# A gated feed-forward kernel: the mirrored value matmul moved between gate and value of the next unit, and a row broadcast done by DMA in place of a matmul

## The chip, the cores and the metric

The kernel runs on one core of one Trainium2 chip. The metric is the time on the device in microseconds (us), as the median of several executions. A profile is one execution; its span (first to last instruction) is about 1.8 us shorter than the time of that execution. I compare ratios to runs of the kernel before made in the same rounds on the same chip, and give the 95% interval.

PE is TensorE's matmul, ACT is ScalarE, DVE is VectorE, POOL is GpSimd, SP is the engine whose queue issues most DMAs.

## The reference

```python
def reference(x, w_gate, w_val, w_out):        # x: 8 x 3008 x 256, float32
    X = np.fft.fft(np.fft.fft(x, axis=1), axis=2).real
    t = X.reshape(8 * 3008, 256)
    g = t @ w_gate                             # 256 x 1536
    silu = g * (1.0 / (1.0 + np.exp(-g)))
    return (silu * (t @ w_val)) @ w_out        # 1536 x 256
```

The kernel folds the second transform into the weights. The first one has a mirror symmetry along the sequence: a column of coefficients P and one of Q give the row k ("plus", P and Q added) and the row M-k ("minus", P and Q subtracted). So one pass over half of the sequence gives both.

## The kernel before

The half sequence is cut into 24 tiles of up to 512 columns, and the 1536 hidden features into 12 blocks of 128. A *unit* is (tile t, block f). For every unit PE makes in PSUM the gate `g` (two matmuls), from which ACT takes the silu for the plus row. A third matmul with `Wm` (it is -2 times `Wq`, but zero for feature row 0) adds onto the same bank and turns `g` into the mirrored gate, and ACT takes its silu too. The value is done the same way in an ordinary unit. In a *split* unit (f = 0, 2, 3, 5, 7, 9 of tiles 2 to 20; 9 of 12 blocks in tiles 21 and 22) the even part `e` and the odd part `o` go to two banks; DVE combines them into both values, and GpSimd, not DVE, multiplies silu and value. As `Wm` leaves out row 0, DVE must add that row of Q times a weight. It needs that row in all 128 partitions: `bc`.

```python
    psG = ctx.enter_context(tc.tile_pool(name="psG", bufs=3, space=bass.MemoryType.PSUM))
    psV = ctx.enter_context(tc.tile_pool(name="psV", bufs=3, space=bass.MemoryType.PSUM))
    # [...]
    def part_a(u):                                    # L700 on
        # [...]
        mm(g, Wp, 0, Pt, True, False)                 # L716 is inside mm
        mm(g, Wq, 0, Qt, False, True)
        if split(u):
            e = psV.tile([P, T], F32, name="v"); mm(e, Wp, 1, Pt, True, True)
            o = psV.tile([P, T], F32, name="v"); mm(o, Wm, 1, Qt, True, True)
            # sg = silu(g) on ACT (L728);  es = bc * w0 + e (DVE, L731)
            # vp = -0.5 * o + es (DVE, L733);  vm = 0.5 * o + es, reversed (DVE, L735)
            # hp = sg * vp (GpSimd, L736)
            return
        # else: v (two matmuls), sg = silu(g) (ACT, L743), hp = sg * v (DVE, L744)

    def part_b(u):
        # gate: one mirror matmul onto g (L753); unless split: one onto v (L753)
        # split: silu (ACT, L757), hm = silu * vm (GpSimd, L758)
        # else:  silu (ACT, L761), hm = silu * v (DVE, L762)
    # [...]
    for i, u in enumerate(units):
        t, f = u
        if f == 0 and split((t, SPLIT[0])):
            ps = psG.tile([P, T], F32, name="g")
            nc.tensor.matmul(ps[:, :w], sel, pq_tiles(t)[1][:, :w], start=True, stop=True)   # L856
            bc[t] = bcp.tile([P, T], F32, name="bc")
            nc.scalar.copy(bc[t][:, :w], ps[:, :w])                                          # L859
        # [...]
        part_a(u)
        if owork:
            owork.run(4)          # 4 matmuls of the output product of the tile before (L676)
        if prev is not None:
            part_b(prev)          # the mirror of the unit BEFORE
        # [...] 4 more output matmuls; then GpSimd's steps that fold the input of later
        # tiles, and the transforms that fill P and Q of later tiles
        prev = u
```

After every 24 output matmuls ACT copies a bank out (`ev`, L682), which falls into the first four of the units 3, 6, 9 and 0.

Of the kernel before, what the change touches and what calls it, by code (L numbers as in the profile page):

```python
# [12 lines left out]
F32 = mybir.dt.float32  # L13
I32 = mybir.dt.int32
BF16 = mybir.dt.bfloat16
AF = mybir.ActivationFunctionType
Alu = mybir.AluOpType
# [14 lines left out]
def kernel(  # L32
# [8 lines left out]
    nc = tc.nc  # L41
    B, M, D = x.shape
    Dff = moe_w_gate.shape[1]
    P = 128
# [4 lines left out]
    nF = Dff // P  # L49
    T = 512  # L50
# [6 lines left out]
    nT = len(wide)  # L57
# [9 lines left out]
    def width(t):  # L67
        return wide[t]

    def tile_of(c):  # L70
        return max(t for t in range(nT) if t0[t] <= c)
# [6 lines left out]
    psG = ctx.enter_context(tc.tile_pool(name="psG", bufs=3, space=bass.MemoryType.PSUM))  # L78
# [6 lines left out]
    Wm = const.tile([P, 2, Dff], BF16, name="Wm")  # L85
# [5 lines left out]
    sel = const.tile([P, P], BF16, name="sel")  # L91
# [22 lines left out]
    def rows_at(b, row, ap):  # L114
        return bass.AP(tensor=x.tensor, offset=(b * M + row) * D, ap=ap)
# [4 lines left out]
    def down_set(b, a, j, L, n):  # L120

        return rows_at(b, R * (a + 1) - 2 * j, [[2 * L * D, n], [-2 * D, L], [1, 2 * D]])
# [3 lines left out]
    def load_a(b, q):  # L126
        X3 = XA.rearrange("p a q d -> p a (q d)")
        return ([lambda h=h: q.dma_start(out=X3[LA * h:LA * (h + 1), 0:4, :],
                                         in_=up_block(b, JA - LA * h, LA)) for h in range(NA)] +
                [lambda a=a: q.dma_start(out=X3[:, 4 + a, :], in_=down_set(b, a, JA, LA, NA)) for a in range(4)])  # L130
# [99 lines left out]
    for hi in range(2):  # L230
        q.dma_start(out=XC3[64 * hi:64 * hi + NCR, 0:2, :],
                    in_=rows_at(0, 2 * (P + 1) - 1 + 2 * hi * R, [[2 * D, NCR], [R * D, 2], [1, 2 * D]]))
    for hi in range(2):
        for a in range(2):
            q.dma_start(out=XC3[64 * hi:64 * hi + NCR, 2 + a, :],
                        in_=down_set(0, 3 - 2 * hi - a, JC, LC, NC_))
    q.dma_start(out=XC0[NCR:64 + NCR + 1:64, 0:2, 1],
                in_=rows_at(0, 0, [[2 * R * D, 2], [R * D, 2], [1, D]]))
# [21 lines left out]
    for i in range(6):  # L260
        ps = psO.tile([P, T], F32, name="o")
# [99 lines left out]
    opposite(0)  # L361
    nc.vector.memset(EOf[:, 1, :, P:P + 1], 0.0)
    nc.vector.memset(Tab[:, :, :, :, NOO - 1:NOO], 0.0)
    nc.vector.memset(sel[0:1, :], 1.0)
    vts(m2, pcol, scalar1=0.0, scalar2=-2.0, op0=Alu.not_equal, op1=Alu.mult)
    vts(sgn, half, scalar1=1.0 / 32, scalar2=1.0, op0=Alu.mult, op1=Alu.add)
    vts(wC, pc, scalar1=float(LC - 1), scalar2=-0.5, op0=Alu.is_equal, op1=Alu.mult)
# [146 lines left out]
    def pq_tiles(t):  # L514
        if t not in ptile:
            w = width(t) + B if t == nT - 1 else T
            ptile[t] = (pqp if t < nT - 1 else const).tile([P, w], BF16, name="Pt")
            qtile[t] = (pqp if t < nT - 1 else const).tile([P, w], BF16, name="Qt")
        return ptile[t], qtile[t]
# [78 lines left out]
    def whole_part(b, part):  # L598
        transform(b, part, (0,))
        transform(b, part, (1,))  # L600
# [15 lines left out]
    sgp = ctx.enter_context(tc.tile_pool(name="sg", bufs=3))  # L616
    sgv = ctx.enter_context(tc.tile_pool(name="sgv", bufs=4))
    esp = ctx.enter_context(tc.tile_pool(name="es", bufs=2))
    bcp = ctx.enter_context(tc.tile_pool(name="bc", bufs=2))
# [73 lines left out]
    hts = {}  # L693
    state = {}
    owork = None

    SPLIT = (0, 2, 3, 5, 7, 9)
    SPLIT_END = (0, 1, 2, 4, 5, 7, 8, 10, 11)
    t_end = tile_of((B - 1) * H) + 1

    bc = {}

    def split(u):

        return 2 <= u[0] < nT - 1 and u[1] in (SPLIT if u[0] < t_end else SPLIT_END)

    def part_a(u):
        t, f = u
        w = width(t) + (B if t == nT - 1 else 0)
        fs = slice(f * P, (f + 1) * P)  # L710
        if f == 0:
            hts[t] = (hp.tile([P, nF, T + B], BF16, name="hp"), hp.tile([P, nF, T], BF16, name="hm"))
        Pt, Qt = pq_tiles(t)

        def mm(ps, Wt, gv, src, start, stop):
            nc.tensor.matmul(ps[:, :w], Wt[:, gv, fs], src[:, :w], start=start, stop=stop,  # L716
                             skip_group_check=True)

        g = psG.tile([P, T], F32, name="g")
        mm(g, Wp, 0, Pt, True, False)  # L720
        mm(g, Wq, 0, Qt, False, True)
        if split(u):
            e = psV.tile([P, T], F32, name="v")
            mm(e, Wp, 1, Pt, True, True)
            o = psV.tile([P, T], F32, name="v")
            mm(o, Wm, 1, Qt, True, True)
            sg = sgv.tile([P, T], F32, name="sgv")
            nc.scalar.activation(sg[:, :w], g[:, :w], AF.Silu)  # L728
            stt = nc.vector.scalar_tensor_tensor
            es = esp.tile([P, T], F32, name="es")  # L730
            stt(es[:, :w], bc[t][:, :w], w0[:, f:f + 1], e[:, :w], op0=Alu.mult, op1=Alu.add)  # L731
            vp = vvp.tile([P, T], F32, name="vv")
            stt(vp[:, :w], o[:, :w], -0.5, es[:, :w], op0=Alu.mult, op1=Alu.add)  # L733
            vm = vvp.tile([P, T], F32, name="vv")
            stt(vm[:, w - 1::-1], o[:, :w], 0.5, es[:, :w], op0=Alu.mult, op1=Alu.add)  # L735
            nc.gpsimd.tensor_tensor(hts[t][0][:, f, :w], sg[:, :w], vp[:, :w], op=Alu.mult)  # L736
            state[u] = (g, vm)
            return
        v = psV.tile([P, T], F32, name="v")
        mm(v, Wp, 1, Pt, True, False)  # L740
        mm(v, Wq, 1, Qt, False, True)
        sg = sgp.tile([P, T], F32, name="sg")
        nc.scalar.activation(sg[:, :w], g[:, :w], AF.Silu)  # L743
        nc.vector.tensor_tensor(hts[t][0][:, f, :w], sg[:, :w], v[:, :w], op=Alu.mult)  # L744
        state[u] = (g, v)

    def part_b(u):
        t, f = u
        w = width(t)
        Pt, Qt = pq_tiles(t)  # L750
        g, v = state.pop(u)
        for gv, ps in ((0, g), (1, v))[:1 if split(u) else 2]:
            nc.tensor.matmul(ps[:, :w], Wm[:, gv, f * P:(f + 1) * P], Qt[:, :w], start=False, stop=True,  # L753
                             skip_group_check=True)
        if split(u):
            sg = sgv.tile([P, T], F32, name="sgv")
            nc.scalar.activation(sg[:, w - 1::-1], g[:, :w], AF.Silu)  # L757
            nc.gpsimd.tensor_tensor(hts[t][1][:, f, :w], sg[:, :w], v[:, :w], op=Alu.mult)  # L758
            return
        sg = sgp.tile([P, T], F32, name="sg")  # L760
        nc.scalar.activation(sg[:, :w], g[:, :w], AF.Silu)  # L761
        nc.vector.tensor_tensor(hts[t][1][:, f, w - 1::-1], sg[:, :w], v[:, :w], op=Alu.mult)  # L762


    slot = {(b, part): max(first_tile[(b, part)] - 1, 0) * nF + 4 for b, part in jobs}
# [10 lines left out]
    for b in range(2, B, 2):  # L776
        u = slot[(b, 0)] - 1
# [8 lines left out]
    def run_loads(n):  # L786
        for _, fn in loads[:n]:
            fn()
        del loads[:n]

    def fold_step(what, i, unit):
        kind, b = what
        q, j = divmod(i, 7)
        if i == 0:
            run_loads(max((k + 1 for k, (w_, _) in enumerate(loads) if w_ == what), default=0))
        if j == 0:
            if kind == "A":
                queue[what] = fold_steps(nc.gpsimd, XA, *coef_a(b), q, slice(0, P))
            else:
                queue[what] = fold_steps(nc.gpsimd, XC, *coef_c(b), q, slice(64 if b == 1 else 0, P))  # L800
        queue[what].pop(0)()
        if q == 1 and j == 1:
            act_at.setdefault(max(unit + 2, 11), []).append(what)
# [15 lines left out]
    for jb in jobs[1:]:  # L819
        u = slot[jb]  # L820
# [28 lines left out]
    prev = None  # L849
    owork = None  # L850
    for i, u in enumerate(units):
        t, f = u
        if f == 0 and split((t, SPLIT[0])):
            ps = psG.tile([P, T], F32, name="g")
            w = width(t)
            nc.tensor.matmul(ps[:, :w], sel, pq_tiles(t)[1][:, :w], start=True, stop=True)  # L856
            bc.pop(t - 2, None)
            bc[t] = bcp.tile([P, T], F32, name="bc")
            nc.scalar.copy(bc[t][:, :w], ps[:, :w])  # L859
        for fn in before.pop(i, ()):  # L860
            fn()
        if i == 10:
            loads[0:0] = ((("A", 1), fn) for fn in load_a(1, nc.sync))
        run_loads(3)
        part_a(u)
        if owork:
            owork.run(4)
        if prev is not None:
            part_b(prev)
            if prev[1] == nF - 1:  # L870
                owork = OWork(prev[0], hts[prev[0]])
                owork.run(4)
        if owork and not (prev is not None and prev[1] == nF - 1):
            owork.run(4)
        for what, j in fold_at.get(i, ()):
            fold_step(what, j, i)
        for what in act_at.pop(i, ()):
            load_next(what)
        if i in job_at:
            whole_part(*job_at[i])  # L880
        prev = u
    while owork.steps:
        owork.run(8)
    part_b(prev)
    owork = OWork(prev[0], hts[prev[0]])
    owork.run(len(owork.steps))

# [29 lines left out]
```

## Time and profile before

| | before |
|---|---|
| median (3 runs) | 693.2 us (692.7 to 694.4) |
| span of the profile | 691.4 us |
| PE busy | 673.5 us |
| GpSimd busy, 150 to 350 us | 49.1, 48.6, 49.8, 49.7 of every 50 us |

Two lines of the page: busy time (share) and number of instructions of each engine, and the engines' shares in the chain of waits that ended last.

```profile
PE 673.5 (97%) x4369; PEld 414.4 (60%) x4369; DVE 517.9 (75%) x925; ACT 433.4 (63%) x765; POOL 593.4 (86%) x577
...
PE 85%; DMA 4%; DVE 4%; issue 3%; POOL 1%; SPq 1%; ACT 1%; ACTq 0%; POOLq 0%; DVEq 0%
```

PE is the limit. A busy PE is not one at full rate, so I also took the start times of all matmuls out of the trace. The Trainium skill ("TensorE: Matmul & The Clock Gate", the table at its head) gives the array clock as up to 2.4 GHz, and in "Wait — 56ns, not 53.3ns?" a gap of 215.7 ns between warm 512-column matmuls. This trace agrees: 0.216 us. I call a *stop* what exceeds columns / 2.4 GHz by over 30 ns. In the kernel before there are 7.4 us of stops between 48 and 106 us (the start-up stop), 8.0 us after that in the units, 13.7 us at the transforms' own matmuls and 5.2 us in the first 48 us.

The stops in the units look like this in the chain of waits, at unit 3 of a tile. The columns are the start in us, the length in us, and what.

```profile
309.28 0.23 PE g L753
309.51 0.04 issue
309.55 0.23 DVE vv L733
309.78 0.38 issue
310.16 0.69 DVE vv L735
310.85 0.04 issue
310.89 0.38 PE v L716
```

The second value matmul of unit 3 (L716, `o`) waits for a PSUM bank, which DVE gives back with the last of its three steps for unit 2 (L735). Without the wait PE would have issued it 0.26 us sooner. It happens in nearly every tile.

What the change will touch on ACT is the distance between a gate and its mirror. In the timeline (start, length, engine, line, instruction, out<-in, and in brackets how long the engine was idle before and who released it):

```profile
306.08 0.38 PE L716 MATMUL g<-Qt,Wq 128*128 128x512 bf16 x1
...
306.50 0.60 ACT L743 ACTIVATE sg<-g 128x512 f32<-128x512 f32 x1 [0.22 <-PE g L716]
...
309.12 0.38 PE L753 MATMUL g<-Qt,Wm 128*128 128x512 bf16 x1
...
309.54 0.60 ACT L761 ACTIVATE sg<-g 128x512 f32<-128x512 f32 x1 [0.43 <-PE g L753]
```

The last gate matmul of unit 1 starts at 306.08, the silu runs from 306.50 to 307.10, and the mirror matmul on the same bank comes at 309.12. ACT may be late by 2 us before PE notices.

Last, the start-up. SP issues DMAs with hardly a pause from 58 to 92 us, and GpSimd is fully busy with folding (L153 and on) and products. The SP queue of the kernel before, two of its lines:

```profile
66.78 2.42 SPq L137 DMA_DIRECT2D XC<-in_x_dram  x6
...
87.61 0.64 SPq L141 DMA_DIRECT2D XC<-in_x_dram  x1
```

and GpSimd there:

```profile
89.66 2.35 POOL L153 TENSOR_TENSOR SDf<-XC 128x1024 f32<-128x1024 f32 x1 [0.28 <-DMA XA<-in_x_dram]
```

The fold that starts at 89.66 had to wait 0.28 us. The profile names an XA load, but its input is XC, whose last load went out at 87.61.

### The profile page before, as it was taken

How to read it: one execution, taken by the hardware profiler on the slowest of the kernel's cores; microseconds unless marked ns; L12 is line 12 of the kernel's file. 1: busy time of each engine (PE TensorE's matmuls, PEld its weight loads, DVE VectorE, ACT ScalarE, POOL GpSimd, SP SyncE). 2: the span in 40 equal slices, each digit the busy share in tenths (PEclk: the TensorE clock that was granted, in tenths of full speed). 3: DMA queues.
4: the chain of work that ended last, by engine and by line, in shares of the span. 5: the costliest groups of instructions: out<-in, count | busy, mean ns of one | idle time of the engine just before them, and what ended most of it. 6: DMA issues, size and time to landing. Idle time of an engine off the chain costs nothing.

```text
span 691.4 us, 13273 instructions
## 1 busy us (share of the span) xinstructions
PE 673.5 (97%) x4369; PEld 414.4 (60%) x4369; DVE 517.9 (75%) x925; ACT 433.4 (63%) x765; POOL 593.4 (86%) x577
## 2 busy tenths in 40 slices
PE   7999979999999999999999999999999999999997
PEld 5446645566556566566665656655665656656676
DVE  8896657677768777777777778777877787788862
ACT  7676546566556566565665656655666656656663
POOL 8998999999999999999997989998999555658920
PEclk9999999999999999999999999999999999999999
DMA  9656362332413313324134111125111011111112
GB/s 225 113 78 131 101 142 74 96 99 61 131 37 90 110 31 105 89 68 132 47 82 117 45 34 46 32 58 140 43 36 46 32 41 37 46 32 47 47 47 70
DMA packets 45567, 52.55 MB, mean 76 GB/s; under 512 B 6290, under 2 KB 33466, under 8 KB 45498
## 3 DMA queue, kind: packets, MB, share of 16 engines
q1 hardware_dynamic: 42314, 49.35, 26.2%
q0 software_dynamic: 3184, 2.36, 2.4%
q8 instruction: 34, 0.56, 0.4%
q14 instruction: 35, 0.29, 0.2%
HBM read 29.39 MB, written 24.65 MB: 78 GB/s over the span
## 4 chain that ended last, share of the span: by engine, by line
PE 85%; DMA 4%; DVE 4%; issue 3%; POOL 1%; SPq 1%; ACT 1%; ACTq 0%; POOLq 0%; DVEq 0%
PE o L676 33%; PE v L716 17%; PE g L716 15%; PE g L753 8%; PE v L753 4%; PE g L567 3%; PE v L567 3%; DVE vv L735 2%; DMA XC<-in_x_dram 2%; DMA XC_108<-in_x_dram 1%; SPq L139 1%; DMA XA<-in_x_dram 1%; DVE vv L733 1%; DMA out_dram<-ev 1%; PE g L856 1%
## 5 line engine op out<-in xcount | busy, mean ns | idle before, releaser
L736 POOL TENSOR_TENSOR hp<-sgv,vv 128x512 bf16<-128x512 f32 (+1 forms) x132 | 167.8, 1272 | 49.8 <-DVE vv L733 38.4
L758 POOL TENSOR_TENSOR hm<-sgv,vv 128x512 bf16<-128x512 f32 (+1 forms) x132 | 167.3, 1272 | 8.5 <-ACT sgv L757 8.1
L676 PE MATMUL o<-Wo,hp 128*128 128x256 bf16 (+2 forms) x1140 | 170.6, 274 | 0.0
L676 PE MATMUL o<-Wo,hm 128*128 128x256 bf16 (+2 forms) x1140 | 169.6, 273 | 0.0
L676 PEld LDWEIGHTS <-hp 128*128 128x128 bf16 (+2 forms) x1140 | 112.3, 99 | 70.9 <-issue 11.3
L676 PEld LDWEIGHTS <-hm 128*128 128x128 bf16 (+2 forms) x1140 | 111.9, 98 | 64.8 <-issue 5.5
L731 DVE SCALAR_TENSOR_TENSOR es<-bc,w_85,v 128x512 f32<-128x512 f32 (+1 forms) x132 | 98.2, 744 | 51.3 <-PE v L716 51.0
L744 DVE TENSOR_TENSOR hp<-sg,v 128x512 bf16<-128x512 f32 (+2 forms) x156 | 103.7, 665 | 31.2 <-ACT sg L743 30.8
L761 ACT ACTIVATE sg<-g 128x512 f32<-128x512 f32 (+2 forms) x156 | 91.1, 584 | 43.1 <-PE g L753 43.0
L762 DVE TENSOR_TENSOR hm<-sg,v 128x512 bf16<-128x512 f32 (+2 forms) x156 | 103.2, 662 | 18.7 <-ACT sg L761 8.6
L743 ACT ACTIVATE sg<-g 128x512 f32<-128x512 f32 (+2 forms) x156 | 90.9, 583 | 41.5 <-PE g L716 39.6
L757 ACT ACTIVATE sgv<-g 128x512 f32<-128x512 f32 (+1 forms) x132 | 78.9, 598 | 53.9 <-PE g L753 41.3
L716 PE MATMUL v<-Pt,Wp 128*128 128x512 bf16 (+2 forms) x288 | 107.9, 375 | 1.6 <-DVE vv L735 1.6
L716 PE MATMUL g<-Pt,Wp 128*128 128x512 bf16 (+2 forms) x288 | 108.3, 376 | 1.0 <-ACT sgv L757 0.9
L716 PE MATMUL g<-Qt,Wq 128*128 128x512 bf16 (+2 forms) x288 | 108.0, 375 | 0.5 <-DVE Qt L580 0.5
L753 PE MATMUL g<-Qt,Wm 128*128 128x512 bf16 (+2 forms) x288 | 108.1, 375 | 0.0
L733 DVE SCALAR_TENSOR_TENSOR vv<-v,es 128x512 f32<-128x512 f32 (+1 forms) x132 | 91.1, 690 | 22.5 <-POOL hp L736 4.6
L728 ACT ACTIVATE sgv<-g 128x512 f32<-128x512 f32 (+1 forms) x132 | 78.7, 596 | 44.8 <-PE g L716 34.9
L735 DVE SCALAR_TENSOR_TENSOR vv<-v,es 128x512 f32<-128x512 f32 (+1 forms) x132 | 89.8, 681 | 8.1 <-POOL hm L758 5.2
L716 PEld LDWEIGHTS <-Wp 128*128 128x128 bf16 x576 | 56.4, 98 | 41.1 <-issue 4.5
L682 ACT COPY ev<-o 128x512 f32<-128x512 f32 x90 | 52.8, 587 | 30.9 <-PE o L676 29.7
L153 POOL TENSOR_TENSOR SDf<-XA 128x1024 f32<-128x1024 f32 x28 | 66.0, 2364 | 3.4 <-DMA XC<-in_x_dram 2.6
(173 smaller groups left out, 736.0 us busy)
## 6 DMA issues: line engine op xcount, KB each, us to landing
out_dram<-ev SPq DMA_DIRECT2D x96, 128.0 KB
XA<-in_x_dram SPq DMA_DIRECT2D x32, 256.0 KB
XA<-in_x_dram SPq DMA_DIRECT2D x112, 64.0 KB
XC<-in_x_dram SPq DMA_DIRECT2D x105, 32.0 KB
XC<-in_x_dram SPq DMA_DIRECT2D x28, 120.0 KB
out_dram<-ev SPq DMA_DIRECT2D x12, 120.0 KB
out_dram<-ev SPq DMA_DIRECT2D x10, 112.0 KB
XA<-in_x_dram SPq DMA_DIRECT2D x1, 1024.0 KB
```

Source lines behind the costliest of these rows:

```text
L676: nc.tensor.matmul(ps[:n, j, :], hts[minus][:, f, c:c + n], Wo[:, f, :], start=(f == 0), stop=(f == nF - 1))
L716: nc.tensor.matmul(ps[:, :w], Wt[:, gv, fs], src[:, :w], start=start, stop=stop, skip_group_check=True)
L731: stt(es[:, :w], bc[t][:, :w], w0[:, f:f + 1], e[:, :w], op0=Alu.mult, op1=Alu.add)
L733: stt(vp[:, :w], o[:, :w], -0.5, es[:, :w], op0=Alu.mult, op1=Alu.add)
L735: stt(vm[:, w - 1::-1], o[:, :w], 0.5, es[:, :w], op0=Alu.mult, op1=Alu.add)
L736: nc.gpsimd.tensor_tensor(hts[t][0][:, f, :w], sg[:, :w], vp[:, :w], op=Alu.mult)
L743: nc.scalar.activation(sg[:, :w], g[:, :w], AF.Silu)
L744: nc.vector.tensor_tensor(hts[t][0][:, f, :w], sg[:, :w], v[:, :w], op=Alu.mult)
L753: nc.tensor.matmul(ps[:, :w], Wm[:, gv, f * P:(f + 1) * P], Qt[:, :w], start=False, stop=True, skip_group_check=True)
L758: nc.gpsimd.tensor_tensor(hts[t][1][:, f, :w], sg[:, :w], v[:, :w], op=Alu.mult)
L761: nc.scalar.activation(sg[:, :w], g[:, :w], AF.Silu)
L762: nc.vector.tensor_tensor(hts[t][1][:, f, w - 1::-1], sg[:, :w], v[:, :w], op=Alu.mult)
```

## The change

The intent is to take the broadcast matmuls off PE (4.5 us) and to issue the value matmuls later, so that DVE has time to free the PSUM banks. The core of the diff:

```diff
-        if f == 0 and split((t, SPLIT[0])):
-            ps = psG.tile([P, T], F32, name="g")
-            nc.tensor.matmul(ps[:, :w], sel, pq_tiles(t)[1][:, :w], start=True, stop=True)
-            bc.pop(t - 2, None)
-            bc[t] = bcp.tile([P, T], F32, name="bc")
-            nc.scalar.copy(bc[t][:, :w], ps[:, :w])
+        if f == (10 if t == 2 else 7) and t + 1 < nT and split((t + 1, SPLIT[0])):
+            bc.pop(t - 1, None)
+            bc[t + 1] = bcp.tile([P, T], BF16, name="bc")
+            w = width(t + 1)
+            nc.sync.dma_start(out=rowd[t + 1:t + 2, :w], in_=pq_tiles(t + 1)[1][0:1, :w])
+            nc.sync.dma_start(out=bc[t + 1][:, :w], in_=rowd[t + 1:t + 2, :w].to_broadcast([P, w]))
 [...]
-        part_a(u)
-        if owork:
-            owork.run(4)
-        if prev is not None:
-            part_b(prev)
+        # (the first tile keeps the old order)
+            gate_b(prev)          # mirror matmul of the gate of the unit before, and its silu
+            if owork:
+                owork.run(4)
+            gate_a(u)             # gate matmuls, silu
+            value_b(prev)         # mirror matmul of the value of the unit before (not split)
             # [...] a new output product starts here after unit 11
+            value_a(u)            # value matmuls, DVE's steps, product
             owork.run(4)
```

`rowd` is a scratch tensor in DRAM. The functions `gate_a`, `value_a`, `gate_b`, `value_b` are the halves of `part_a` and `part_b`, with the same instructions.

More of the change, by code (lines that the diff above doesn't have):

```diff
@@ L363 @@
     nc.vector.memset(Tab[:, :, :, :, NOO - 1:NOO], 0.0)
-    nc.vector.memset(sel[0:1, :], 1.0)
     vts(m2, pcol, scalar1=0.0, scalar2=-2.0, op0=Alu.not_equal, op1=Alu.mult)
@@ L699 @@
     t_end = tile_of((B - 1) * H) + 1
+    rowd = tc.dram_tile([nT, T], BF16, name="rowd")
     bc = {}
@@ L705, in split, with gate_a @@
         return 2 <= u[0] < nT - 1 and u[1] in (SPLIT if u[0] < t_end else SPLIT_END)
-    def part_a(u):
+    def gate_a(u):
         t, f = u
@@ L721, in part_a, with value_a, mm @@
         mm(g, Wq, 0, Qt, False, True)
+        sg = (sgv if split(u) else sgp).tile([P, T], F32, name="sgv" if split(u) else "sg")
+        nc.scalar.activation(sg[:, :w], g[:, :w], AF.Silu)
+        state[u] = (g, sg)
+    def value_a(u):
+        t, f = u
+        w = width(t) + (B if t == nT - 1 else 0)
+        fs = slice(f * P, (f + 1) * P)
+        Pt, Qt = pq_tiles(t)
+        g, sg = state[u]
+        def mm(ps, Wt, gv, src, start, stop):
+            nc.tensor.matmul(ps[:, :w], Wt[:, gv, fs], src[:, :w], start=start, stop=stop,
+                             skip_group_check=True)
         if split(u):
@@ L726, in part_a @@
             mm(o, Wm, 1, Qt, True, True)
-            sg = sgv.tile([P, T], F32, name="sgv")
-            nc.scalar.activation(sg[:, :w], g[:, :w], AF.Silu)
             stt = nc.vector.scalar_tensor_tensor
@@ L741, in part_a, with mirror, gate_b @@
         mm(v, Wq, 1, Qt, False, True)
-        sg = sgp.tile([P, T], F32, name="sg")
-        nc.scalar.activation(sg[:, :w], g[:, :w], AF.Silu)
         nc.vector.tensor_tensor(hts[t][0][:, f, :w], sg[:, :w], v[:, :w], op=Alu.mult)
         state[u] = (g, v)
-    def part_b(u):
+    def mirror(u, gv, ps):
         t, f = u
         w = width(t)
-        Pt, Qt = pq_tiles(t)
-        g, v = state.pop(u)
-        for gv, ps in ((0, g), (1, v))[:1 if split(u) else 2]:
-            nc.tensor.matmul(ps[:, :w], Wm[:, gv, f * P:(f + 1) * P], Qt[:, :w], start=False, stop=True,
-                             skip_group_check=True)
+        nc.tensor.matmul(ps[:, :w], Wm[:, gv, f * P:(f + 1) * P], pq_tiles(t)[1][:, :w], start=False, stop=True,
+                         skip_group_check=True)
+    def gate_b(u):
+        t, f = u
+        w = width(t)
+        g, v = state[u]
+        mirror(u, 0, g)
         if split(u):
@@ L758, in part_b, with value_b @@
             nc.gpsimd.tensor_tensor(hts[t][1][:, f, :w], sg[:, :w], v[:, :w], op=Alu.mult)
-            return
-        sg = sgp.tile([P, T], F32, name="sg")
-        nc.scalar.activation(sg[:, :w], g[:, :w], AF.Silu)
-        nc.vector.tensor_tensor(hts[t][1][:, f, w - 1::-1], sg[:, :w], v[:, :w], op=Alu.mult)
+        else:
+            sg = sgp.tile([P, T], F32, name="sg")
+            nc.scalar.activation(sg[:, :w], g[:, :w], AF.Silu)
+            state[u] = (sg, v)
+    def value_b(u):
+        t, f = u
+        w = width(t)
+        sg, v = state.pop(u)
+        if not split(u):
+            mirror(u, 1, v)
+            nc.vector.tensor_tensor(hts[t][1][:, f, w - 1::-1], sg[:, :w], v[:, :w], op=Alu.mult)
     slot = {(b, part): max(first_tile[(b, part)] - 1, 0) * nF + 4 for b, part in jobs}
@@ L852 @@
         t, f = u
-        if f == 0 and split((t, SPLIT[0])):
-            ps = psG.tile([P, T], F32, name="g")
-            w = width(t)
-            nc.tensor.matmul(ps[:, :w], sel, pq_tiles(t)[1][:, :w], start=True, stop=True)
-            bc.pop(t - 2, None)
-            bc[t] = bcp.tile([P, T], F32, name="bc")
-            nc.scalar.copy(bc[t][:, :w], ps[:, :w])
+        if f == (10 if t == 2 else 7) and t + 1 < nT and split((t + 1, SPLIT[0])):
[4 more added lines that the diff above has]
+            nc.sync.dma_start(out=bc[t + 1][:, :w], in_=rowd[t + 1:t + 2, :w].to_broadcast([P, w]))
         for fn in before.pop(i, ()):
@@ L864 @@
         run_loads(3)
-        part_a(u)
-        if owork:
-            owork.run(4)
-        if prev is not None:
-            part_b(prev)
+        if i < nF:
+            gate_a(u)
+            value_a(u)
+            if prev is not None:
+                gate_b(prev)
+                value_b(prev)
+        else:
+            gate_b(prev)
+            if owork:
+                owork.run(4)
+            gate_a(u)
+            value_b(prev)
             if prev[1] == nF - 1:
                 owork = OWork(prev[0], hts[prev[0]])
-                owork.run(4)
-        if owork and not (prev is not None and prev[1] == nF - 1):
+            value_a(u)
             owork.run(4)
@@ L883 @@
         owork.run(8)
-    part_b(prev)
+    gate_b(prev)
+    value_b(prev)
     owork = OWork(prev[0], hts[prev[0]])
```

## The prediction

> **What bounds the kernel now.** TensorE. The engine table gives PE 673.5 of 691.4 us busy; the chain of waits is 85% PE; from 150 to 650 us every stretch of 50 us has PE above 49.4. In the timeline a 512-column matmul follows the last by 0.216 us, a 256-column one by 0.109. The Trainium skill ("TensorE: Matmul & The Clock Gate", "Wait — 56ns, not 53.3ns?") gives 215.7 ns as the warm full-rate gap, so PE streams and only removed columns or gaps help. I compared matmul starts with that rate between 100 and 660 us: gaps that a reordering can reach sum to 7.7 us. They are one stop of 0.26 us in nearly every tile (unit f=3: its second value matmul waits for the PSUM buffer that VectorE's third value step of unit 2 frees; the chain shows this 25 times) and 0.06 us at unit 0 after the broadcast matmul. A separate stop of 7.3 us lies at 77 to 98 us, where GpSimd is behind, then waits for XC loads.
>
> **What the change removes.** 21 broadcast matmuls, 0.216 us each: 4.5 us, all on the chain. 21 ACT copies of 0.59 us, off the chain. Later value matmuls give VectorE time to free PSUM buffers: up to 7.7 us.
>
> **What it adds.**
> 1. A tight loop of ACT and PE. Before, the gate's mirror matmul came a unit after its silu. Now 1.08 us (unit ahead split) or 1.30 lie between gate and mirror matmul of one unit. From the timeline: silu starts 0.42 to 0.47 us after the last gate matmul, takes 0.60, PE resumes 0.04 later: 1.06 to 1.11. It just fits. But where an output eviction (ACT starts 0.48 us apart) stands between the two silus, at units 3, 6, 9, 0, the loop is 2.08 us against a unit of 1.95 (split ahead) or 2.17: 0.13 us lost at units 3 and 6, four times per tile in the last split tiles: about 6 us in all.
> 2. ACT's waits for GpSimd buffers (some 10 us from 100 to 600 us in the wait list; GpSimd is 97 to 99% busy from 95 to 350) were absorbed by that slack; part now reaches PE: 3 us.
> 3. Two DMAs on SP, the second waiting for the first to land. A 4 KB XC load took 1.95 us to land in the chain; the skill ("DMA: Bandwidth & Descriptors", "Anatomy of one DMA") gives about 2 us of fixed cost. Later SP mostly idles. But at 65 us (tile 1, unit 7) SP issues without a pause until 92, and the XC load that GpSimd waits for at 89.6 would land some 2 us later: 2 us.
>
> **Sum.** -4.5 - 7.7 + 6 + 3 + 2: about -1 us, the added items the less certain; if they half vanish, -7. I say 690 us (-0.5%), range 683 to 697. Chances: faster by over 2% 0.04, within 2% 0.93, slower 0.03.
>
> **What would show it.** Right: no broadcast matmul and no bc copy; the chain's VectorE pieces at unit 3 gone; in their place gate-mirror matmuls waiting for ACT silus at units 3 and 6 (about 0.1 us each, the chain passing through silu and eviction); SP standing some 2 us in each tile between row store and broadcast load; PE idle at 77 to 98 us grown by 1 to 3 us. Wrong: PE gaps at units 3 and 6 absent (then 683 or below), or VectorE stops remaining.
>
> **What would make it wrong.** ACT latency under load above the timeline's 0.42: every unit then loses 0.05 us or more, 15 us in all. GpSimd becoming the limit from 100 to 350 us. Or the start-up stop shrinking because value matmuls come later: up to 7 us better.

## The result, and the profile after

The change has a median of 697.5 us (696.7 to 699.0, 4 runs) against 693.7 us for the kernel before (4 runs). The ratio is 1.0058, interval 1.0036 to 1.0081: slower by 0.6%, and half a microsecond outside of the stated range. (Ratios are the mean time of one kernel's fast runs over that of the other's of the same rounds, so not quite the ratio of the medians.) The profiled run is the slowest of the four (699.0 us); a repeat further below has a profile of a 696.2 us run.

The same two lines of the page:

```profile
PE 674.9 (97%) x4348; PEld 412.4 (59%) x4348; DVE 515.8 (74%) x924; ACT 413.7 (59%) x744; POOL 592.9 (85%) x577
...
PE 80%; POOL 6%; DMA 4%; issue 3%; DVE 3%; SPq 2%; ACT 1%; DVEq 0%; POOLq 0%; ACTq 0%
```

The chain of unit 3 has changed its cause. No VectorE piece stands there any more; PE waits at the mirror matmul of the gate (L761). The timeline at unit 3, again only the lines of the loop:

```profile
318.10 0.38 PE L761 MATMUL g<-Qt,Wm 128*128 128x512 bf16 x1
...
318.58 0.60 ACT L772 ACTIVATE sgv<-g 128x512 f32<-128x512 f32 x1 [0.70 <-PE g L761]
...
318.97 0.38 PE L716 MATMUL g<-Qt,Wq 128*128 128x512 bf16 x1
...
319.07 0.58 ACT L681 COPY ev<-o 128x512 f32<-128x512 f32 x1
...
319.54 0.62 ACT L723 ACTIVATE sgv<-g 128x512 f32<-128x512 f32 x1
...
320.20 0.38 PE L761 MATMUL g<-Qt,Wm 128*128 128x512 bf16 x1
```

The mirror matmul of unit 2 starts at 318.10 and releases ACT at 318.58. The output eviction follows at 319.07, the silu of unit 3 only at 319.54, though its last gate matmul started at 318.97. That silu ends at 320.16, and the mirror matmul of unit 3 starts at 320.20, 2.10 us after that of unit 2. At full rate it would have been 1.95. The stop is 0.15 us, and it comes twice in a tile. In the list of waits (us in total, times, longest) only the longer ones of this kind are named:

```profile
PE g L761 <- ACT sgv L723: 9.4, 5, 3.5
PE g L761 <- ACT sg L723: 2.4, 3, 1.3
```

One of the long ones, at 291 us:

```profile
285.21 4.68 POOL L153 TENSOR_TENSOR SDf<-XA 128x1024 f32<-128x1024 f32 x2
...
289.84 1.28 POOL L749 TENSOR_TENSOR hp<-sgv,vv 128x512 bf16<-128x512 f32 x1
...
291.15 0.60 ACT L723 ACTIVATE sgv<-g 128x512 f32<-128x512 f32 x1 [1.65 <-POOL hp L749]
...
291.80 0.38 PE L761 MATMUL g<-Qt,Wm 128*128 128x512 bf16 x1 [1.73 <-ACT sgv L723]
```

GpSimd takes two folds in a row (4.68 us). The silu of the gate has no free buffer until GpSimd's next product is done (289.84 on), so it starts at 291.15, and PE waits for it. The kernel before had such waits of ACT too, but two microseconds of slack behind them.

In the start-up, SP:

```profile
68.72 0.23 SPq L881 DMA_DIRECT2D rowd<-Qt  x1
70.43 0.35 SPq L882 DMA_DIRECT2D bc<-rowd  x1
70.83 2.03 SPq L137 DMA_DIRECT2D XC<-in_x_dram  x6
...
90.61 0.64 SPq L141 DMA_DIRECT2D XC<-in_x_dram  x1
```

and GpSimd:

```profile
92.52 2.35 POOL L153 TENSOR_TENSOR SDf<-XC 128x1024 f32<-128x1024 f32 x1 [2.68 <-DMA XC<-in_x_dram]
```

Between the row's store (68.72) and its broadcast load (70.43) SP stands still. The last XC load goes out 3.0 us later than before (90.61), and the fold starts 2.9 us later, after a wait of 2.68 us. Not all of this is the standstill's: the output stores ahead of it went out at 67.07, and at 65.61 in the kernel before, so SP was 1.5 us late already. The repeat of the change (e10, below) is a warning. SP stands still there too, from 66.9 to 67.94, and yet:

```profile
87.62 0.64 SPq L141 DMA_DIRECT2D XC<-in_x_dram  x1
89.52 2.35 POOL L153 TENSOR_TENSOR SDf<-XC 128x1024 f32<-128x1024 f32 x1 [0.92 <-DMA XC<-in_x_dram]
```

The last XC load and the fold come as early as in the kernel before (87.61, 89.66), and GpSimd's products until 105 us too (the last one starts at 104.77, before at 104.92). The start-up stop is still 2.1 us longer than before. The late XC load can't be the reason for those 2.1 us; I have no run that shows what is. The stretch from 77 to 106 us (columns: bounds, length, then busy us and number of instructions of PE, PE's weight loads, DVE, ACT, GpSimd, then granted clock, DMA share, GB/s), first of the kernel before:

```profile
77.00:106.00 29.00, 24.22 (x149) 14.13 (x147) 18.18 (x31) 13.85 (x26) 28.49 (x26) 0.94 0.54 133
```

and after:

```profile
77.00:106.00 29.00, 21.01 (x109) 11.76 (x108) 13.79 (x21) 10.64 (x20) 26.09 (x24) 0.82 0.48 131
```

PE's clock falls further. After the stop that ends at 87.84 the matmuls start 0.43 us apart for three microseconds (to 90.92). The skill ("TensorE: Matmul & The Clock Gate", "What's actually happening") describes this half rate after an idle window and the return after some 3.4 us of work.

This table counts PE's time by matmul starts, for all kernels whose trace is complete (each sums to the time from the first to the last matmul). "Streaming" is columns at 2.4 GHz plus gaps under 30 ns.

| us in the profiled run | streaming | until 48 us | 48 to 106 us | transforms | units after 106 us |
|---|---|---|---|---|---|
| before | 652.1 | 5.2 | 7.4 | 13.7 | 8.0 |
| the change (699.0 us) | 647.5 | 5.4 | 12.7 | 14.3 | 12.7 |
| the change, repeat (696.2 us) | 647.5 | 5.5 | 9.5 | 14.5 | 12.7 |
| order only | 651.9 | 5.5 | 6.5 | 14.5 | 13.9 |
| DMA only | 647.6 | 5.4 | 9.4 | 13.9 | 11.6 |
| gates together | 647.7 | 6.4 | 11.6 | 15.1 | 8.4 |
| eviction later | 647.6 | 5.4 | 8.2 | 14.5 | 7.7 |
| three mends | 647.7 | 6.0 | 4.4 | 16.4 | 5.5 |
| three mends, tile 2 not split | 649.0 | 5.9 | 0.5 | 16.3 | 4.9 |
| before, tile 2 not split | 653.2 | 6.6 | 0.0 | 14.1 | 8.0 |

The removed columns came off in full (4.6 us). The old stops in the units (8.0 us) are gone, but new ones of 12.7 us took their place, and the start-up stop is longer by 5.3 us in one profile of the change and by 2.1 in the other.

### The profile page after: what moved, and what is told of

The parts are those of the page before. It is cut to its first block, busy times and chain, and to the rows that moved or that the text cites. A ratio compares the mean times of both kernels' runs of the same rounds, so it can differ in the third digit from the quotient of the medians.

```text
span 697.2 us, 13316 instructions
## 1 busy us (share of the span) xinstructions
PE 674.9 (97%) x4348; PEld 412.4 (59%) x4348; DVE 515.8 (74%) x924; ACT 413.7 (59%) x744; POOL 592.9 (85%) x577
## 4 chain that ended last, share of the span: by engine, by line
PE 80%; POOL 6%; DMA 4%; issue 3%; DVE 3%; SPq 2%; ACT 1%; DVEq 0%; POOLq 0%; ACTq 0%
PE o L675 30%; PE g L716 14%; PE v L734 14%; PE g L761 8%; PE v L761 4%; DMA XA<-in_x_dram 4%; PE g L566 3%; PE v L566 3%; POOL SDf L153 2%; POOL hm L773 1%; POOL hp L749 1%; DVE vv L746 1%; DMA out_dram<-ev 1%; PE v L542 1%; PE g L542 1%
## 5 line engine op out<-in xcount | busy, mean ns | idle before, releaser
L761 PE MATMUL g<-Qt,Wm 128*128 128x512 bf16 (+2 forms) x288 | 108.4, 376 | 12.0 <-ACT sgv L723 9.4
L744 DVE SCALAR_TENSOR_TENSOR es<-bc,w,v 128x512 f32<-128x512 bf16 (+1 forms) x132 | 97.6, 740 | 0.3 <-PE v L734 0.3
L761 PE MATMUL v<-Qt,Wm 128*128 128x512 bf16 (+2 forms) x156 | 58.2, 373 | 2.0 <-DVE hp L755 2.0
L734 PE MATMUL v<-Qt,Wq 128*128 128x512 bf16 (+2 forms) x156 | 58.5, 375 | 0.0
```

Source lines behind the costliest of these rows:

```text
L734: nc.tensor.matmul(ps[:, :w], Wt[:, gv, fs], src[:, :w], start=start, stop=stop, skip_group_check=True)
L744: stt(es[:, :w], bc[t][:, :w], w0[:, f:f + 1], e[:, :w], op0=Alu.mult, op1=Alu.add)
L761: nc.tensor.matmul(ps[:, :w], Wm[:, gv, f * P:(f + 1) * P], pq_tiles(t)[1][:, :w], start=False, stop=True, skip_group_check=True)
```

## The experiments

Theory A is that of the prediction, sharpened by the trace: the new order takes away the slack between a gate's silu and its mirror matmul, so that evictions and GpSimd's delays on ACT reach PE; the DMAs gain the broadcast matmuls and lose at start-up. Theory B: the order is a gain and the two DMAs lose everything, by holding up SP. Every kernel gave right results.

### Order only (e1_order_only)

```diff
 (against the change)
-        [the two row DMAs]
+        [the broadcast matmul and the ACT copy at f == 0, as before]
```

> The new order with the old broadcast (matmul and ACT copy), no row DMAs. Theory A (the loop of gate silu, eviction, mirror silu costs PE 0.15 us twice a tile, about 7 us, and GpSimd waits that now reach PE about 4 us, against 7.6 us of removed value stops): slower than before by 2 to 5 us, 696 to 699 us; the 0.15 us stops at units 3 and 6 stay; GpSimd's wait for the XC load near 90 us falls from 2.7 us to under 0.6. Theory B (the loss is the two row DMAs holding SP up; the order itself is a gain): 5 us or more faster than before, 689 or below.

Measured: 701.1 us, ratio 1.0098 (1.0073 to 1.0123). Theory B falls. The new order with the old broadcast is slower than the change, 6.8 us slower than before by the ratio, somewhat more than the 2 to 5 us that theory A gave. The 0.15 us stops are there, and now 55 of them instead of 39: the copy of `bc` on ACT at unit 0 stands in the loop together with an eviction and makes a third stop in a tile. GpSimd's fold near 90 us has no wait for XC of note, as expected; the one wait of 1.1 us for XC in this profile ends at 64.19 us, where the other profiles have one too.

### DMA only (e2_dma_only)

```diff
 (against the kernel before)
-        [the broadcast matmul and the ACT copy at f == 0]
+        [the two row DMAs of the change]
```

> The old order with the new broadcast by two DMAs. Theory A: the 4.5 us of broadcast matmuls go, 2 to 3 us come back at 77 to 100 us because the XC load lands later; 690 to 693 us, 1 to 4 us faster than before; the value stops of 0.26 us stay; no stops at gate-mirror matmuls. Theory B: slower than before by 3 us or more.

Measured: 695.5 us, ratio 1.0023 (1.0001 to 1.0045). Neither expectation held: it is slower by some 1.6 us, where theory A had a gain of 1 to 4. The table shows why. The streaming fell by 4.5 us, but the stops in the units rose by 3.6, from 8.0 to 11.6, and the start-up stop by 2.0. In the kernel before, at unit 0:

```profile
331.89 0.38 PE L856 MATMUL g<-Qt,sel 128*128 128x512 bf16 x1
...
332.06 0.69 DVE L762 TENSOR_TENSOR hm<-sg,v 128x512 bf16<-128x512 f32 x1 [0.40 <-PE o L676]
...
332.53 0.38 PE L716 MATMUL v<-Pt,Wp 128*128 128x512 bf16 x1
...
332.80 0.38 PE L716 MATMUL v<-Qt,Wm 128*128 128x512 bf16 x1
```

The second value matmul of unit 0 (332.80) starts when DVE has finished `hm` of the last unit (332.06 plus 0.69), which frees its bank. The broadcast matmul stood in the time in which PE would have waited, and the stop left over was 0.06 us. Without it, the chain of waits of this experiment:

```profile
333.70 0.23 PE g L753
333.93 0.02 issue
333.95 0.60 ACT sg L761
334.56 0.02 issue
334.58 0.70 DVE hm L762
335.28 0.04 issue
335.32 0.38 PE v L716
```

It runs from the mirror matmul of the gate (L753) through ACT's silu and DVE's product to the value matmul, and nothing on PE makes it shorter. The stop at unit 0 is now 0.27 us. Matmul and stop together took 0.216 + 0.057 us before, and the stop alone takes 0.273 now: in the old order the removed matmul was worth nothing. GpSimd's longest wait for XC in this profile looks like the start-up loss, and is not:

```profile
66.88 4.67 POOL L153 TENSOR_TENSOR SDf<-XA 128x1024 f32<-128x1024 f32 x2 [3.94 <-DMA XC<-in_x_dram]
```

It ends at 66.88 us, and the first row store goes out at 69.10. So the row DMAs did not make this wait, which takes 2.60 us in the kernel before and 1.1 to 2.8 us in order only and the two profiles of the change: the loads of the start-up differ that much from run to run. The last XC load goes out at 89.93, 2.3 us later than before, but SP was 1.8 us behind before the row store. How much of the 2.0 us the two DMAs cost is not shown.

### Gates together (e3_gates_together)

```diff
 (against the change)
             gate_b(prev)
-            if owork:
-                owork.run(4)
             gate_a(u)
+            if owork:
+                owork.run(4)
             value_b(prev)
```

> The change, with the first four output matmuls of a unit moved behind the gate matmuls, so that gate and its mirror matmul are 0.44 us further apart. Theory A: the 0.15 us stops at units 3 and 6 are gone and part of the GpSimd waits are absorbed again: 686 to 691 us, 7 to 11 us faster than the change. Theory B: within 1.5 us of the change, 696 to 699.

Measured: 693.3 us, ratio 0.9988 (0.9967 to 1.0010): about 5 us better than the change by the ratios, with one of the 0.15 us stops left. The gain is smaller than the 7 to 11 us expected. The long stops behind GpSimd did not shrink (7.4 us, part of it at half clock around 292 us), and the start-up stop was 11.6 us in this profile.

### Eviction later (e4_evict_later)

```diff
 (against the change; the order on PE is untouched)
             gate_b(prev)
+            held = []
             if owork:
-                owork.run(4)
+                owork.run(4, held)      # the eviction is put off
             gate_a(u)
+            for fn in held:
+                fn()
             value_b(prev)
```

> The change, PE order untouched; only the output eviction that falls between the mirror silu and the next gate silu is issued behind the gate silu on ACT. Theory A (eviction between the two silus is what makes the loop too long): the 0.15 us stops fall to 0.05 or less, 690 to 693 us. Rival C (ACT is simply late by its load, wherever the eviction stands): the stops stay or move to the neighbouring units, 696 to 699.

Measured: 692.8 us, ratio 0.9984 (0.9962 to 1.0006), and the stops are as theory A had them. All 0.15 us stops are gone and 25 of 0.04 us are left. In the timeline at unit 3:

```profile
313.20 0.38 PE L765 MATMUL g<-Qt,Wm 128*128 128x512 bf16 x1
...
313.68 0.60 ACT L776 ACTIVATE sgv<-g 128x512 f32<-128x512 f32 x1 [0.70 <-PE g L765]
...
314.54 0.60 ACT L727 ACTIVATE sgv<-g 128x512 f32<-128x512 f32 x1 [0.27 <-PE g L720]
...
315.04 0.58 ACT L681 COPY ev<-o 128x512 f32<-128x512 f32 x1
...
315.19 0.38 PE L765 MATMUL g<-Qt,Wm 128*128 128x512 bf16 x1
```

The silu of unit 3 now starts 0.86 us after that of the mirror, not 0.96, and the eviction follows it. From one mirror matmul to the next it takes 1.99 us instead of 2.10. Two places exchanged on an engine that is busy 60% of the time are worth 5 us. Rival C falls.

### Store early (e5_store_early)

```diff
 (against the change)
+        first = 4 if t == 1 else 10 if t == 2 else 7
+        [store the row of tile t + 1 at f == first]
+        [load it at f == first + 3, in tile 2 at f == 11]
```

> The change, with the row's store issued three units (in tile 2 one unit) ahead of its broadcast load, so that SP need not stand still for its landing. If SP's standstill at 68 us is what moved the XC load: GpSimd's wait for XC near 90 us falls from 2.7 to under 1 us and the run is 2 to 3 us faster than the change (ratio to before 1.001 to 1.004). Rival (the start-up stop is set by GpSimd's own work): under 1 us faster, ratio 1.005 or more.

Measured: 695.8 us, ratio 1.0025 (1.0007 to 1.0043), about 2.3 us better than the change. The difference of the two ratios has an interval of some 0.3 to 4.3 us, so the gain is just clear of the noise. GpSimd's wait for XC near 90 us is 1.10 us in this profile, not under 1; the repeat of the change, without this mend, has 0.92. So the time speaks for a cost of SP's standstill, but the path from it to PE is not shown.

### Gate ahead (e7_gate_ahead)

```diff
 (against the change)
+            gate_a(u)
             gate_b(prev)
             if owork:
                 owork.run(4)
-            gate_a(u)
             value_b(prev)
```

> The change, with the gate matmuls of a unit moved ahead of the mirrored gate matmul of the unit before: a whole unit lies again between a gate's silu and its mirror matmul, and the value matmuls stay where the change put them. Theory A (what the new order lost is the slack of that silu): the 0.15 us stops are gone and the stops on GpSimd between 150 and 300 us fall from 4 us to under 1.5; 9 to 12 us faster than the change, ratio to before 0.988 to 0.993. Rival (0.44 us of slack was enough, the rest is GpSimd's own limit): like the run with the gates together, 0.997 to 1.000.

Measured: 693.9 us, ratio 0.9990 (0.9973 to 1.0007): 4.7 us better than the change, not 9 to 12. The stops in the units did fall, from 12.7 to about 5 us, none of them at 0.15. But the transforms' stops rose to some 18 us, and the start-up stop was 10 us. I have not tested why the transforms lose; a wait of the transform's first matmul for a DVE value step (1.3 us) appears in the list of waits, and mirrored products come later in this order. (In the traces of this and the next two kernels and of the one above, 67 of 4348 matmul records are missing; each leaves a gap of one matmul, which I left out by its size. Their sums are rough, so they are not in the table.)

### More buffers (e8_more_buffers)

```diff
 (against the change)
-    sgv = ctx.enter_context(tc.tile_pool(name="sgv", bufs=4))
+    sgv = ctx.enter_context(tc.tile_pool(name="sgv", bufs=6))
-    vvp = ctx.enter_context(tc.tile_pool(name="vv", bufs=4))
+    vvp = ctx.enter_context(tc.tile_pool(name="vv", bufs=5))
```

(A first form with 6 and 6 did not fit into SBUF.)

> The change with 6 instead of 4 buffers for the split units' silus and 5 instead of 4 for their values. If the long stops between 100 and 300 us come from too few buffers between ACT and GpSimd: those 4 us fall to under 1.5 and the start-up stop shrinks by up to 2; 3 to 6 us faster than the change, ratio 0.997 to 1.002; the 0.15 us stops stay. Rival (GpSimd's throughput is the limit there): under 1.5 us faster.

Measured: 694.3 us, ratio 1.0003 (0.9987 to 1.0018), 3.8 us better than the change. The stops in the units other than those of 0.15 us and less fell from 6.1 to 2.9 us, and the 0.15 us stops stayed. So GpSimd has the throughput for those stretches; what lacked was room for its backlog. (I have not tried more buffers in the kernel before.)

### Gate ahead and store early (e9_ahead_store)

> Both: the gate matmuls ahead and the row's store early. The two gains should add: 11 to 14 us faster than the change, ratio to before 0.985 to 0.990, faster than before by 7 to 10 us; what remains is the stop of about 7 us at 77 to 100 us.

Measured: 692.1 us, ratio 0.9969 (0.9947 to 0.9992). It is the two edits above together. It is 6.2 us better than the change, so the gains nearly add (4.7 and 2.3), from the smaller gain that the gate ahead gave.

### The change again (e10_change_again)

> The change itself once more, beside the others of this batch: ratio to before 1.003 to 1.008, as on record.

Measured: 697.9 us (696.2 to 699.8), ratio 1.0053 (1.0034 to 1.0073). The stops in the units are the same to 0.1 us in both profiles. The start-up stop is not: 9.5 us against 12.7.

### Three mends (e11_three_mends)

The edits of "eviction later", "store early" and "more buffers" in one kernel.

> The change with all three mends: the eviction behind the gate silu, the row's store early, 6 and 5 buffers between ACT, VectorE and GpSimd. If the three losses named so far (the 0.15 us stops, the waits on GpSimd's buffers, SP's standstill) are all that the change lost, they add up: stops after 106 us below 4 us (8.0 before, 12.7 in the change), 9 to 13 us faster than the change, ratio 0.987 to 0.993. Rival (the start-up stop swallows what is gained elsewhere, because GpSimd's work there is what has to be finished): 0.995 or more.

Measured: 686.6 us (686.5 to 686.9), ratio 0.9889 (0.9873 to 0.9906). Singly, the mends had gained 7.4, 3.3 and 5.5 thousandths on the change (differences of ratios, with 1.0058 for the change). The sum is 16.2, and together they gained 16.4 against the repeat in the same rounds (1.0053 - 0.9889). The gains add, and the rival falls. (The single mends ran on other chips than the three together; the change itself agrees between two of them, 1.0058 and 1.0053.) In detail it was not as expected. 5.5 us of stops remain in the units, not under 4, the transforms' stops rose to 16.4 us, and the start-up stop fell to 4.4 us, lower than "eviction later" (8.2) or either profile of the change has it. So the times add better than the pieces do, and why the start-up stop fell only with the three together is not shown. The stretch from 77 to 106 us:

```profile
77.00:106.00 29.00, 25.48 (x166) 15.04 (x165) 20.67 (x40) 15.34 (x28) 28.23 (x26) 1.00 0.54 131
```

PE does 166 matmuls there in place of 109 (130 in the repeat, clock 0.94), and its clock no longer falls. The runs now lie within 0.4 us of each other, while those of the change differ by 3.6 us. It fits that the spread comes from the start-up stop and from whether PE's clock falls in it; only one run of each kernel was profiled, so this is not shown. The record has the mean granted clock of every run, and in each kernel's runs the slower ones tend to have the lower clock: 696.2 us at 0.996 and 699.8 at 0.993 in the repeat, 690.1 us at 1.000 and 694.3 at 0.993 in "eviction later".

### Tile 2 not split (e12_split_from_3, e13_before_from_3)

```diff
-        return 2 <= u[0] < nT - 1 and u[1] in (SPLIT if u[0] < t_end else SPLIT_END)
+        return 3 <= u[0] < nT - 1 and u[1] in (SPLIT if u[0] < t_end else SPLIT_END)
```

The first is added to the three mends, the second to the kernel before alone.

> The same with tile 2 not split, so that GpSimd has 12 products of 1.27 us less to do between 77 and 106 us and PE six matmuls of 0.216 us more. If that stop is GpSimd's load: it falls from some 9 us to under 3 and the run is 4 to 7 us faster than the three mends, ratio 0.978 to 0.986. If it is late DMA data: within 2 us of the three mends.

> The kernel before, with only tile 2 not split: the share of the last step that has nothing to do with the change. If GpSimd's load makes the stop: 7.4 us of stops fall to under 2, plus 1.3 us of matmuls: ratio 0.992 to 0.996.

Measured: 683.5 us, ratio 0.9858 (0.9838 to 0.9879), and 688.5 us, ratio 0.9913 (0.9898 to 0.9928). The stop between 48 and 106 us fell from 4.4 to 0.5 us and from 7.4 us to nothing. So the stop came through GpSimd's products, of which a tile without split units has 12 of 1.27 us less. In the kernel before it was GpSimd's load, with 28.49 of 29 us busy from 77 to 106. In the change GpSimd also waited (26.09 busy), and this edit does not tell load and wait apart, as without those products PE would feel neither. The three mends with tile 2 not split:

```profile
77.00:106.00 29.00, 28.75 (x190) 17.26 (x189) 17.43 (x36) 17.24 (x31) 23.09 (x23) 1.00 0.56 143
```

Its gain on the mends is 2.2 us (3.1 thousandths), short of the 4 to 7 us expected and hardly over the 2 us named for late DMA data: the mends had already brought that stop down from 9.5 to 4.4 us. The edit helps the kernel before by 0.9% on its own (0.4 to 0.8% was expected), so this part has nothing to do with the change. The three mends and this edit together are the fastest kernel, 1.4% faster than before.

## Why the prediction was right or wrong

- **PE bound, at full rate.** Right: streaming is 652 of 691 us, and only removed columns and removed stops counted.
- **The removed value stops, 7.7 us.** Right: 8.0 us of old stops in the units, none left in the change.
- **The broadcast matmuls, 4.5 us, "all on the chain".** Right inside the change, where streaming fell by 4.6 us. Wrong as a statement about the old kernel: DMA only shows that there they filled a wait, and taking them alone brought 3.6 us of stops back.
- **The tight loop of ACT and PE, 6 us.** Right in mechanism, place and nearly in size. The prediction had 0.13 us at units 3 and 6; the trace has 39 stops of 0.15 us and 11 of 0.04 to 0.06, 6.5 us. Moving the eviction proved the cause.
- **GpSimd's waits that reach PE, 3 us.** Right in mechanism, half of the size. The other stops in the units sum to 6.1 us in the change (0.7 us of such in the kernel before outside of the two stop patterns), and more buffers took 3.1 us of them away. In the trace, the stops at 179.0, 291.8 and 645.2 us (3.3 us) lie directly behind an ACT silu that waited for a GpSimd product; for the smaller ones it is argued.
- **SP's standstill, 2 us.** SP does stand still, 1.7 us from store to load at 68.7 us. The rest of the path (a late XC load, a late fold, a longer stop) is seen in one profile, where the XC load was 3.0 us later and the stop 5.3 us longer, but 1.5 us of the delay lay before the row store, and the clock was 0.82, which the sum had no term for. In the repeat the stop is 2.1 us longer with the XC load on time. That this is the predicted size is luck. Storing the row early won 2.3 us; how, stays open.
- **The step that failed: added item 2, "part now reaches PE: 3 us", and after it the discount, "the added items the less certain; if they half vanish, -7. I say 690 us".** In place of 3 us the units have 6.1 us of stops beside the loop's. The start-up, 2 us in the sum, was 2.1 and 5.3 us, and the transforms and the first 48 us, 0.8 to 1.1 us, had no term. The sum stood at 692 us, and it was then moved down by 2 because costs seemed less certain than gains. The runs showed the opposite: none of the three costs vanished and two were larger. With what the profiles measured the sum is -4.6 (streaming) - 8.0 + 12.7 (6.5 loop, 6.1 GpSimd, to rounding) + 2.1 to 5.3 (start-up) + 0.8 to 1.1 (transforms and the first 48 us) = +3.3 to +6.1 us (of the profiled runs, whose spans are 3.0 and 5.8 us longer); the measured median difference is +3.7 us. The uncertainty of a cost has two sides: a loop that needs 1.06 to 1.11 us and has 1.08 can only lose from every further delay.
- **What was missing from the prediction** is that two of the three costs came from one thing, the lost slack between a gate's silu and its mirror, and that they could be mended one by one. With the mends, the kernel is 1.1% faster than before instead of 0.6% slower. How much of this the kernel before would gain from more buffers alone was not run.

## What to carry to other kernels

When a reordering shortens the distance between a producer and the engine that must answer it, write the round trip down from the trace (here 0.48 + 0.60 + 0.04 us) and add every instruction that the answering engine may put in between; an engine that is 60% busy can still stop PE twice in a tile. An instruction that fills a wait costs nothing, so before counting a removed one as a gain, look at what the next instruction would wait for without it. And do not discount a cost because it is less certain than the gain beside it.

## What the Trainium skill lacked or had wrong

- "DMA: Bandwidth & Descriptors", "Anatomy of one DMA": it gives about 2.0 us of fixed cost, a fit for the GpSimd path. Here, for a row of at most 1 KB stored to DRAM from the SP queue, the dependent load was issued 1.40 us after the store (median of 21 tiles, 1.13 to 2.17).
- "TensorE: Matmul & The Clock Gate", "HAM oscillation — how this bites in real kernels": the rule it states is no idle gap above about 3.4 us. In the kernel before, half rate followed stops of 1.1 and 2.1 us with 0.6 us of matmuls between them; in "eviction later" stops of 2.9, 1.2, 2.0 and 2.1 us brought none (granted clock 1.00). The rule as stated does not tell which happens; whether the page's free-running window explains it, no run here shows.
- "ScalarE: Activation LUTs", "What ACT_TABLE_LOAD costs": from its 186 ns + 0.833 ns an element I estimate 0.61 us for 512 elements, and the trace has 0.60. With its overlap of 93 ns between ACTIVATEs the estimate is 0.52 us from start to start; they are 0.49 apart here (318.58, 319.07).
- On "Perfetto Trace Analysis" I found nothing on missing matmul records: four of the traces lack 67 of 4348, and each leaves a gap of 0.22 us that looks like a stop.
- The same page gives no time for the way from a matmul to the ACT instruction that waits for it: 0.42 to 0.48 us from the start of the last 512-column matmul to the start of the silu, and 0.04 us from the silu's end to the next matmul.
